# A gated linear attention with an expert layer on one core: logits made token by token, tables on GpSimd, the running state added by TensorE, first loads reordered

## The chip, the cores and the metric

The kernel runs on one core of one Trainium2 chip. Its time is the device time of one execution in microseconds (us), lower is better; the kernel before was run three times, and the median is given with the lowest and the highest. Beside these runs stands one execution taken by the profiler.

The engines are called PE (TensorE, matrix products; PEld its weight loads), DVE (VectorE), ACT (ScalarE), POOL (GpSimd) and SP (SyncE, which here only starts transfers).

## What is computed

An attention with a decaying state, and behind it a layer that sends each token to the one expert with the largest logit.

```
q, k, v, alpha: (4, 8, 768, 48)          batch, heads, sequence, width
for t in range(768):
    state = alpha[t][:, None] * state + outer(k[t], v[t])      # per batch and head
    y[t]  = q[t] @ state
x = y, tokens by (head, width): (3072, 384)
logits = x @ w_gate + modality_bias[modality_id]               # 8 experts
e = argmax(logits);  gate = softmax(logits)[e]
out[token] = gate * (relu(x[token] @ w1[e]) @ w2[e])           # 384 -> 1024 -> 384
```

## The kernel before, in words

**Chunks.** The tokens are cut into 24 chunks of 128 (NU), six for each of the four sequences (NC). A chunk holds all 8 heads. The host lays the inputs out: `turned` has keys, queries and decays with the width on the partitions (two heads side by side, 112 partitions, 1600 columns, 700 KB a chunk), and `rowsv` has the values with the tokens on the partitions, each head's 48 columns padded to 64 with zeros (256 KB a chunk).

**Loads.** `load` (L125) issues a chunk's two transfers on SP's queue. For chunk 0 the block comes in three parts (decays, keys, queries). Three chunks are loaded ahead (PF), there are four block buffers (TN) and six value buffers (VT).

**One step of the attention loop** (L812 to L844), step s of 24. The order is written out by hand for PE, DVE, ACT and POOL. Different chunks are in different stages:
- DVE: `decay(s)` (a scan over the decays backwards into the PSUM tile GF, L233, two small instructions, and keys times GF, L239, as `kh`), then `decay_back(s)` (a second scan, L243, and queries times GF, L245, as `qh`).
- PE and ACT: `natural(s-1)` turns the keys (L256), `rows(s-3)` turns the outputs into rows and stores them to `xd` (L326, L331), `state(s-2)` multiplies the queries with the state T1 carried in (L288), `scores(s-1)` makes keys times queries (L268), which ACT copies and POOL masks (L272, L273), `outputs(s-2)` multiplies the masked scores with the values (L295, ACT copy L303 to `yt`), `update(s-1)` makes keys times values (L313).
- `update` goes on with an ACT copy (L315), a POOL addition of the carried state T1 (L317), and a POOL multiplication by the chunk's decay, which gives the next T1 (L319).
- Every second step two chunks get their logits: `logits` (L338) multiplies the gate weights as the stationary operand, four narrow column groups, so that experts lie on partitions; ACT copies (L340); one step on `logits_rows` turns both back with two transposes (L346) and DVE sums the four groups into `L` (L348).

PSUM tiles named `tr` share three buffers in turn; `kv` (GF's name) and `y` have one, `sc` two. In the last part of the attention the logits use `kv` (`turns`) and the routing uses `sc` (`place`).

**Routing beside it.** `bias_table` (L201) makes the table `bt` of each token's bias from its modality, mostly on DVE, in pieces from step 5 on. In five groups of chunks (`GROUPS`: 0 to 5, 6 to 11, 12 to 15, 16 to 19, 20 to 23) `route_flow` (L398) adds the bias (L409), takes the largest logit (L410 to L414, giving the one-hot `oh`), counts with PE how many tokens before it went to the same expert (L417 to L424), and makes each token's slot: `r1`, `hr`, `lo`, `hi`, and the table `OL` of 128 columns a chunk (L437). After 16 and after 20 chunks `route_early` (L494) picks the fullest expert, has its weights loaded (`weights`, L618, four transfers of 768 KB on SP's queue), and looks up 256 of its tokens (`OHE`, L518 and L524; PE L531; `places`), which `gather` (L650) fetches on POOL's queue. These flows are generators; `advance()` runs one more piece of each flow at two places of a step: behind `decay` and behind `decay_back`.

**Hand-over.** After the loop the last scores, outputs and logits are interleaved by hand with the last pieces of routing and with the first products of the first expert (`first_inputs`, `first_unit`, L121).

**Experts.** Blocks of 256 or 512 tokens are multiplied with their expert's weights. Both operands are split into a high and a low part on ACT and DVE and multiplied in three products (L955 to L957 and L974 to L976), with weight loads and gathers beside it.

Of the kernel before, what the change touches and what calls it, by code (L numbers as in the profile page):

```python
# [21 lines left out]
P = 128  # L22
# [3 lines left out]
W = 64 + D  # L26
# [39 lines left out]
def attention_moe(ctx: ExitStack, tc: tile.TileContext, q, k, v, alpha, mid, wg, mb, w1, w2, turned, rowsv, small, out):  # L66
# [25 lines left out]
    for i in range(NV):  # L92
        t = ac.tile([P, H, 64], F32, name=f"vt{i}")
        VT.append(t)
# [29 lines left out]

    def load(i):  # L125
        if i:
            sp.dma_start(TN[i % NB], turned[i])
        else:
            for c in (slice(2 * KW, RW), slice(0, KW), slice(KW, 2 * KW)):
                sp.dma_start(TN[0][:, c], turned[0, :, c])  # L130
        sp.dma_start(VT[i % NV], rowsv[i])

    wgs = cp.tile([P, ND, E], F32, name="wgs")
    for i in range(PF):
        load(i)
# [24 lines left out]
    for i in range(3):  # L160
        t = ac.tile([W, NP, 64], F32, name=f"T1{i}")
        pool.memset(t[:, :, D:], 0.0)
        T1.append(t)
    bhi = ac.tile([P, 1], F32, name="bhi")
# [36 lines left out]
    def bias_table():  # L201
        mf = ac.tile([NU, P], F32, name="mf")
        vec.tensor_copy(mf, mi[:, :, 0])
        yield
        mp = ps.tile([P, NU], F32, name="sc", bufs=2)
        pe.transpose(mp, mf, ident[:NU, :NU])
        mt = ac.tile([P, NU], F32, name="mt")
        vec.tensor_copy(mt, mp)
        tmp = ac.tile([P, NU, E], F32, name="btt")
        for m in range(NM):  # L210
            yield
            sel = ac.tile([P, NU], F32, name=f"msel{m}")
            vec.tensor_scalar(sel, mt, float(m), None, op0=ALU.is_equal)
            vec.tensor_tensor(
# [5 lines left out]
            if m:  # L220
                vec.tensor_tensor(bt, bt, tmp, op=ALU.add)

# [83 lines left out]
    def update(i):  # L306
# [8 lines left out]
        act.copy(S1, kv)  # L315
        if i % NC > 0:
            pool.tensor_tensor(S1, S1, T1[i % 3][:, :, :D], op=ALU.add)  # L317
# [15 lines left out]
    def logits(i):  # L333

        lt = ps.tile([P, 2, P], F32, **turns)
        for n in range(NP):
            g, h = divmod(n, 2)
            pe.matmul(lt[32 * n : 32 * n + 32], wgp[:, g, h], st[i, "yt"][:, :, g, h], start=True, stop=True)  # L338
        ls = sb.tile([P, 2, P], F32, name="lts")
        act.copy(ls, lt)  # L340
        st[i, "l"] = ls

    def logits_rows(i):
        lp = ps.tile([P, 2, P], F32, **turns)
        for c in range(2):
            pe.transpose(lp[:, c], st[i, "l"][:, c], ident)  # L346
        z = slice(i - 1, i + 1)
        vec.tensor_reduce(L[:, z], lp.rearrange("p c (j e) -> p c e j", e=32)[:, :, :E], axis=AX.X, op=ALU.add)  # L348
# [880 lines left out]
```

## Time and profile before

| | |
|---|---|
| median of 3 runs | 363.36 us (361.44 to 364.71) |
| profiled execution, its own time | 362.08 us |
| its span, first to last instruction | 360.3 us |
| busy in the span: PE, PEld | 333.0 us, 288.9 us |
| busy in the span: DVE, ACT, POOL | 223.8 us, 177.7 us, 156.2 us |
| mean granted PE clock | 0.968 of full speed |
| first scan of the first step | 4.26 us |
| read from and written to HBM | 53.69 MB, 9.50 MB |

A row in order of time gives start, length, engine, line, operation, what it writes and reads, the shapes, how many instructions were merged, and in brackets how long the engine stood idle before it and what ended that. Merged rows overlap a little: an instruction's length reaches past the start of the next one, so distances between starts are what an engine needs. A row of a group gives the count, the busy time in us, the mean of one in ns, and idle time ahead of it. In the rows by slices each digit is a tenth of busy time in one of 40 equal slices of 9 us.

### The profile page before, as it was taken

How to read it: one execution, taken by the hardware profiler on the slowest of the kernel's cores; microseconds unless marked ns; L12 is line 12 of the kernel's file. 1: busy time of each engine (PE TensorE's matmuls, PEld its weight loads, DVE VectorE, ACT ScalarE, POOL GpSimd, SP SyncE). 2: the span in 40 equal slices, each digit the busy share in tenths (PEclk: the TensorE clock that was granted, in tenths of full speed). 3: DMA queues.
4: the chain of work that ended last, by engine and by line, in shares of the span. 5: the costliest groups of instructions: out<-in, count | busy, mean ns of one | idle time of the engine just before them, and what ended most of it. 6: DMA issues, size and time to landing. Idle time of an engine off the chain costs nothing. (4 is left out here: it accounts for less than half of the span.)

```text
span 360.3 us, 8600 instructions
## 1 busy us (share of the span) xinstructions
PE 333.0 (92%) x3378; PEld 288.9 (80%) x3378; DVE 223.8 (62%) x438; ACT 177.7 (49%) x344; POOL 156.2 (43%) x197
## 2 busy tenths in 40 slices
PE   6599889997986989998999999999999999999993
PEld 2487678675775868898988998899899888988992
DVE  5799999999999875978466226604560555036400
ACT  2477677684875554446355144515542544154410
POOL 8378366573835532075556127123702571120021
PEclk9589999998999699999999999999999999999998
DMA  8999998699792949779474336333641573110011
GB/s 227 256 258 285 274 284 227 197 277 241 222 253 67 313 151 308 258 254 318 142 243 147 109 104 225 94 126 133 196 132 67 159 253 90 46 44 6 1 45 51
DMA packets 29333, 63.78 MB, mean 177 GB/s; under 512 B 3369, under 2 KB 14792, under 8 KB 29284
## 3 DMA queue, kind: packets, MB, share of 16 engines
q1 hardware_dynamic: 25140, 53.40, 49.7%
q0 software_dynamic: 4000, 9.68, 7.9%
q8 instruction: 28, 0.46, 0.6%
q14 instruction: 21, 0.17, 0.2%
q10 hardware_dynamic: 144, 0.07, 0.1%
HBM read 53.69 MB, written 9.50 MB: 175 GB/s over the span
## 5 line engine op out<-in xcount | busy, mean ns | idle before, releaser
L921 POOL DMA_INDIRECT out_dram<-os,odx x23 | 23.5, 1020 | 102.9 <-ACT os L989 93.9
L955 PE MATMUL sc<-w2H,hH 128*128 128x384 f32 x192 | 65.2, 340 | 0.0
L957 PE MATMUL sc<-w2H,hL 128*128 128x384 f32 x192 | 64.3, 335 | 0.0
L956 PE MATMUL sc<-w2L,hH 128*128 128x384 f32 x192 | 64.3, 335 | 0.0
L799 DVE TENSOR_TENSOR w1L<-w1r,w1H 128x768 fp32r<-128x768 f32 x24 | 22.0, 956 | 65.2 <-ACT w1H L797 65.2
L273 POOL TENSOR_SCALAR_AFFINE_SELECT scT<-scT 128x512 f32<-128x512 f32 x48 | 38.5, 825 | 46.1 <-ACT scT L272 46.1
L974 PE MATMUL tr<-xH,w1H 128*128 128x512 f32 (+1 forms) x144 | 53.9, 374 | 0.0
L976 PE MATMUL tr<-xH,w1L 128*128 128x512 f32 (+1 forms) x144 | 53.6, 372 | 0.0
L975 PE MATMUL tr<-xL,w1H 128*128 128x512 f32 (+1 forms) x144 | 53.5, 372 | 0.0
L791 DVE SCALAR_TENSOR_TENSOR hL<-tr,hH 128x512 fp32r<-128x512 f32 x47 | 32.4, 689 | 30.8 <-ACT hH L789 30.8
L789 ACT ACTIVATE hH<-tr 128x512 fp32r<-128x512 f32 x47 | 28.1, 598 | 43.0 <-PE tr L976 41.7
L989 ACT ACTIVATE os<-sc,gg 128x384 f32<-128x384 f32 x23 | 13.4, 582 | 66.8 <-PE sc L957 40.7
L658 POOL DMA_INDIRECT gg<-gd,idx x25 | 27.1, 1083 | 26.7 <-DMA gd<-gs 19.7
L955 PEld LDWEIGHTS sc<-w2H,hH 128*128 128x128 f32 x192 | 36.1, 188 | 1.1 <-issue 1.0
L956 PEld LDWEIGHTS sc<-w2L,hH 128*128 128x128 f32 x192 | 36.1, 188 | 0.0
L957 PEld LDWEIGHTS sc<-w2H,hL 128*128 128x128 f32 x192 | 36.1, 188 | 0.0
L233 DVE TENSOR_TENSOR_SCAN kv<-tn,DR 112x512 f32<-112x512 f32 x24 | 32.6, 1357 | 5.1 <-DMA tn<-in_turned_dram 4.7
L272 ACT COPY scT<-sc 128x512 f32<-128x512 f32 x48 | 25.8, 589 | 18.9 <-PE sc L268 18.9
L268 PE MATMUL sc<-qh,kh 48*64 48x128 f32 x768 | 29.5, 290 | 4.7 <-DVE qh L245 2.9
L652 POOL DMA_INDIRECT xg<-xd,idx x25 | 26.7, 1067 | 14.8 <-DVE vals L488 8.1
L243 DVE TENSOR_TENSOR_SCAN kv<-tn,DF 112x512 f32<-112x512 f32 x24 | 31.4, 1309 | 0.3
L268 PEld LDWEIGHTS sc<-qh,kh 48*64 48x64 f32 x768 | 24.5, 145 | 8.0 <-DVE qh L245 3.2
(245 smaller groups left out, 599.1 us busy)
## 6 DMA issues: line engine op xcount, KB each, us to landing
tn<-in_turned_dram SPq DMA_DIRECT2D x23, 700.0 KB, 6.6
w1r<-in_moe_w_dram SPq DMA_DIRECT2D x16, 768.0 KB, 4.9
w2r<-in_moe_w_dram SPq DMA_DIRECT2D x16, 768.0 KB, 6.1
vt<-in_rowsv_dram SPq DMA_DIRECT2D x24, 256.0 KB, 6.7
xd<-xs SPq DMA_DIRECT2D x24, 192.0 KB, 6.4
tn<-in_turned_dram SPq DMA_DIRECT2D x2, 224.0 KB, 4.1
xg<-xd,idx POOLq DMA_INDIRECT x25, 4.3
gg<-gd,idx POOLq DMA_INDIRECT x25, 3.7
```

The costliest lines, as they stand in the source:

```text
L233: vec.tensor_tensor_scan(GF[:, ::-1], alphas(i, 1, KW + 1)[:, ::-1], DR[:, ::-1], 0.0, op0=ALU.mult, op1=ALU.max)
L243: vec.tensor_tensor_scan(GF, alphas(i, 0, KW), DF[i % 2], 0.0, op0=ALU.mult, op1=ALU.add)
L268: pe.matmul(pp[g][z, j], kh[r, j, z], qh[r, j], start=True, stop=True)
L273: pool.affine_select(s, s, [[0, NP], [1, P]], ALU.is_ge, 0.0, base=0, channel_multiplier=-1)
L789: act.activation(hH, hp, AF.Relu)
L791: vec.scalar_tensor_tensor(hL, hp, 0.0, hH.bitcast(F32), op0=ALU.max, op1=ALU.subtract)
L955: pe.matmul(op, hH[:, us] if f is None else hH[:, f, us], wH, start=first, stop=False)
L956: pe.matmul(op, hH[:, us] if f is None else hH[:, f, us], wL, start=False, stop=False)
L957: pe.matmul(op, hL[:, us] if f is None else hL[:, f, us], wH, start=False, stop=final)
L974: pe.matmul(hp, wH[:, d, fs], XH[:, d, :n], start=(d == 0), stop=False)
L975: pe.matmul(hp, wH[:, d, fs], XL[:, d, :n], start=False, stop=False)
L976: pe.matmul(hp, wL[:, d, fs], XH[:, d, :n], start=False, stop=(d == ND - 1))
```

## The change

- **Loads.** Chunk 0's block in parts as before; then chunk 1's decays and keys, chunk 0's values, chunk 1's queries, chunk 1's values, and then chunk 2 as a whole.
- **Values unpadded.** The host no longer pads; a chunk's values are 192 KB. The tile has 64 more columns, set to zero once by POOL (six small memsets). `outputs` still reads 64 columns for each head: the upper 16 are now the next head's values. They land in rows of the output tile that `rows` leaves out and for which the gate weights are zero.
- **Logits.** The output tile `yt` is the stationary operand, eight products of 128 columns by 8 in a group of two chunks; the result has tokens on partitions. ACT's copy, the two transposes and DVE's sum go. `logits_rows` is one DVE addition of the product and the bias into `L`, at the end of the same step. L409 goes. Each group of chunks starts one step earlier.
- **Tables.** `bias_table` runs once in step 1, its two copies on ACT and its five other instructions on POOL. `lo` is made as a float; in the groups 0 to 5, 6 to 11 and 12 to 15 `OL` is made by POOL, one instruction for a chunk.
- **State.** PE adds T1 by a product with the identity ahead of the eight key-value products, all into one PSUM group; POOL's addition L317 goes.
- **Where the pieces run.** A flow says with `yield PEQ` that its next piece begins on PE; such a piece is now put behind `scores` and ahead of `outputs`. The `gather` of an early expert stands directly behind its `places`. In the hand-over one `next(early)` goes, as the group of chunks 16 to 19 is one piece further.

```diff
+    def load_part(i, z):
+        c = (slice(0, KW), slice(KW, 2 * KW), slice(2 * KW, RW))[z]
+        sp.dma_start(TN[i][:, c], turned[i, :, c])
+    def load_rows(i):
+        sp.dma_start(VT[i % NV][:, :DM], rowsv[i])
     def load(i):
-        if i:
-            sp.dma_start(TN[i % NB], turned[i])
-        else:
-            for c in (slice(2 * KW, RW), slice(0, KW), slice(KW, 2 * KW)):
-                sp.dma_start(TN[0][:, c], turned[0, :, c])
-        sp.dma_start(VT[i % NV], rowsv[i])
+        sp.dma_start(TN[i % NB], turned[i])
+        load_rows(i)
-    for i in range(PF):
-        load(i)
+    for z in (2, 0, 1):
+        load_part(0, z)
+    load_part(1, 2)
+    load_part(1, 0)
+    load_rows(0)
+    load_part(1, 1)
+    load_rows(1)
+    load(2)
...
+    for t in VT:
+        pool.memset(t[:, DM:], 0.0)
...
     def bias_table():
-        vec.tensor_copy(mf, mi[:, :, 0])
-        yield
+        act.copy(mf, mi[:, :, 0])
         pe.transpose(mp, mf, ident[:NU, :NU])
-        vec.tensor_copy(mt, mp)
+        act.copy(mt, mp)
         for m in range(NM):
-            yield
-            vec.tensor_scalar(sel, mt, float(m), None, op0=ALU.is_equal)
-            vec.tensor_tensor(
+            pool.tensor_scalar(sel, mt, float(m), None, op0=ALU.is_equal)
+            pool.tensor_tensor(
...
             if m:
-                vec.tensor_tensor(bt, bt, tmp, op=ALU.add)
+                pool.tensor_tensor(bt, bt, tmp, op=ALU.add)
...
     def outputs(i):
-                vt[:, 2 * j + g],
+                vt[:, (2 * j + g) * D : (2 * j + g) * D + 64],
...
     def update(i):
+        if i % NC > 0:
+            pe.matmul(kv, ident[:W, :W], T1[i % 3][:, :, :D], start=True, stop=False)
         for h in range(H):
-            pe.matmul(kv[r, h // 2], kn[:, h // 2, r], vt[:, h, :D], start=True, stop=True)
+            pe.matmul(kv[r, h // 2], kn[:, h // 2, r], vt[:, h * D : (h + 1) * D], start=(i % NC == 0), stop=(i % NC == 0 or h >= H - 2))
         act.copy(S1, kv)
-        if i % NC > 0:
-            pool.tensor_tensor(S1, S1, T1[i % 3][:, :, :D], op=ALU.add)
...
     def logits(i):
-        lt = ps.tile([P, 2, P], F32, **turns)
-        for n in range(NP):
-            g, h = divmod(n, 2)
-            pe.matmul(lt[32 * n : 32 * n + 32], wgp[:, g, h], st[i, "yt"][:, :, g, h], start=True, stop=True)
-        ls = sb.tile([P, 2, P], F32, name="lts")
-        act.copy(ls, lt)
-        st[i, "l"] = ls
+        lp = ps.tile([P, 2, E], F32, **turns)
+        for c in range(2):
+            for n in range(NP):
+                g, h = divmod(n, 2)
+                pe.matmul(lp[:, c], st[i, "yt"][:, c, g, h], wgp[:, g, h, :E], start=(n == 0), stop=(n == NP - 1))
+        st[i, "l"] = lp
     def logits_rows(i):
-        lp = ps.tile([P, 2, P], F32, **turns)
-        for c in range(2):
-            pe.transpose(lp[:, c], st[i, "l"][:, c], ident)
         z = slice(i - 1, i + 1)
-        vec.tensor_reduce(L[:, z], lp.rearrange("p c (j e) -> p c e j", e=32)[:, :, :E], axis=AX.X, op=ALU.add)
+        vec.tensor_tensor(L[:, z], st[i, "l"], bt[:, z], op=ALU.add)
...
-    def route_flow(t0, t1):
+    def route_flow(t0, t1, side=False):
-        vec.tensor_tensor(L[:, s], L[:, s], bt[:, s], op=ALU.add)
         vec.tensor_reduce(mx[:, s], L[:, s], axis=AX.X, op=ALU.max)
         vec.tensor_tensor(ls[:, s], L[:, s], wide(mx), op=ALU.subtract)
+        if side:
+            yield
...
-        yield
+        yield PEQ
         rp = ps.tile([P, n, E], F32, **place)
...
-        vec.tensor_scalar(lo[:, s], r1[:, s], P - 1, None, op0=ALU.bitwise_and)
+        vec.scalar_tensor_tensor(lo[:, s], hr[:, s], -float(P), r1[:, s], op0=ALU.mult, op1=ALU.add)
-        vec.tensor_tensor(OL[:, s], over(ioh, P), wide(lo, P), op=ALU.is_equal)
+        if side:
+            for t in range(t0, t1):
+                pool.tensor_scalar(OL[:, t], ioh, lo[:, t : t + 1], None, op0=ALU.is_equal)
+        else:
+            vec.tensor_tensor(OL[:, s], over(ioh, P), wide(lo, P), op=ALU.is_equal)
...
     def route_early(s):
-        yield
+        yield PEQ
         cnt = ps.tile([P, E], F32, **place)
...
         weights(s, mete[0:1, s : s + 1])
-        yield
+        yield PEQ
         tp = ps.tile([P, 2], F32, **place)
...
         places(tp, slice(UE * s, UE * s + UE))
+        gather(s, early_cols(s), row(n))
...
+    def advance(spot):
+        for f in list(flows):
+            tag, seen = flows[f]
+            if (tag == PEQ) != (spot == PEQ) or seen == (now["s"], 2):
+                continue
+            go(f, spot)
...
         decay(s)
         if live(s - 1) and (s - 1) % NC < NC - 1:
             natural(s - 1)
         if live(s - 3):
             rows(s - 3)
-        if live(s - 4) and s % 2:
-            logits_rows(s - 4)
-        advance()
+            if (s - 3) % 2:
+                logits(s - 3)
+        advance(1)
         decay_back(s)
-        if s < NU - 1:
-            advance()
-        if s % 2:
-            groups(s - 4)
+        advance(2)
+        if live(s - 3) and (s - 3) % 2:
+            logits_rows(s - 3)
+            groups(s - 3)
         if s == 5:
-            start(bias_table())
             half_index()
-        if live(s - 3) and (s - 3) % 2:
-            logits(s - 3)
         guard(s)
         if live(s - 2):
             state(s - 2)
         if live(s - 1):
             scores(s - 1)
+        if s == 1:
+            bias_table()
+        advance(PEQ)
         if live(s - 2):
             outputs(s - 2)
         if live(s - 1):
             update(s - 1)
...
     next(early)
     logits(L0 - 2)
-    next(early)
     state(L0 - 1)
```

More of the change, by code (lines that the diff above doesn't have):

```diff
@@ L92, in attention_moe @@
     for i in range(NV):
-        t = ac.tile([P, H, 64], F32, name=f"vt{i}")
+        t = ac.tile([P, DM + 64], F32, name=f"vt{i}")
         VT.append(t)
@@ L202, in bias_table @@
         mf = ac.tile([NU, P], F32, name="mf")
-        vec.tensor_copy(mf, mi[:, :, 0])
-        yield
-        mp = ps.tile([P, NU], F32, name="sc", bufs=2)
+        act.copy(mf, mi[:, :, 0])
+        mp = ps.tile([P, NU], F32, name="tr", bufs=3)
         pe.transpose(mp, mf, ident[:NU, :NU])
         mt = ac.tile([P, NU], F32, name="mt")
-        vec.tensor_copy(mt, mp)
+        act.copy(mt, mp)
         tmp = ac.tile([P, NU, E], F32, name="btt")
         for m in range(NM):
-            yield
             sel = ac.tile([P, NU], F32, name=f"msel{m}")
-            vec.tensor_scalar(sel, mt, float(m), None, op0=ALU.is_equal)
-            vec.tensor_tensor(
+            pool.tensor_scalar(sel, mt, float(m), None, op0=ALU.is_equal)
+            pool.tensor_tensor(
                 tmp if m else bt,
@@ L358, in logits_pe @@
             pe.matmul(lp, xc[:, c], wgs[:, c], start=(c == 0), stop=(c == ND - 1))
-        vec.tensor_copy(L[:, i], lp)
+        vec.tensor_tensor(L[:, i], lp, bt[:, i], op=ALU.add)
     mx = cp.tile([P, NU], F32, name="mx")
@@ L379, in attention_moe @@
     r1 = cp.tile([P, NU], I32, name="r1")
-    lo = cp.tile([P, NU], I32, name="lo")
+    lo = cp.tile([P, NU], F32, name="lo")
     ls = cp.tile([P, NU, E], F32, name="ls")
@@ L389, in attention_moe @@
     turns = {"name": "tr", "bufs": 3}
+    PEQ = "pe"
     def route_begin():
@@ L749, in group_flow @@
     def group_flow(t0, t1):
-        yield from route_flow(t0, t1)
+        yield from route_flow(t0, t1, t1 < EARLY[-1])
         if t1 in EARLY:
@@ L753, in group_flow @@
             yield from route_early(e)
-            gather(e, early_cols(e), row(t1))
             if e == NA - 1:
@@ L759, in group_flow, with go @@
                     gather_gates(e, early_cols(e), row(t1))
-    flows = []
-    def advance():
+    flows, now = {}, {}
+    def advance(spot):
         for f in list(flows):
-            if next(f, f) is f:
-                flows.remove(f)
-    def start(f):
-        flows.append(f)
-        if next(f, f) is f:
-            flows.remove(f)
-    def finish():
-        while flows:
-            advance()
+            tag, seen = flows[f]
+            if (tag == PEQ) != (spot == PEQ) or seen == (now["s"], 2):
+                continue
+            go(f, spot)
+    def go(f, spot):
+        try:
+            flows[f] = (next(f), (now["s"], spot))
+        except StopIteration:
+            del flows[f]
     def live(i):
@@ L782, in groups @@
             if after == i:
-                start(group_flow(t0, t1))
+                go(group_flow(t0, t1), 2)
     hpool = {}
@@ L817, in attention_moe @@
             sp.dma_start(gd[MID : MID + 1], zr[:, 0:1])
+        now["s"] = s
         decay(s)
@@ L822, in attention_moe @@
             rows(s - 3)
-        if live(s - 4) and s % 2:
-            logits_rows(s - 4)
-        advance()
+            if (s - 3) % 2:
+                logits(s - 3)
+        advance(1)
         decay_back(s)
-        if s < NU - 1:
-            advance()
-        if s % 2:
-            groups(s - 4)
+        advance(2)
+        if live(s - 3) and (s - 3) % 2:
+            logits_rows(s - 3)
+            groups(s - 3)
         if s == 5:
-            start(bias_table())
             half_index()
-        if live(s - 3) and (s - 3) % 2:
-            logits(s - 3)
         guard(s)
@@ L1197, in laid_out @@
     turned[:, :, 2 * KW : 3 * KW] = a.reshape(NU, W, KW)
-    rowsv = np.zeros((NU, P, H, 64), np.float32)
-    rowsv[..., :D] = v.reshape(B, H, NC, P, D).transpose(0, 2, 3, 1, 4).reshape(NU, P, H, D)
+    rowsv = np.ascontiguousarray(v.reshape(B, H, NC, P, D).transpose(0, 2, 3, 1, 4)).reshape(NU, P, DM)
     small = np.zeros((P, P + NM * E), np.float32)
```

## The prediction

> **What bounds the kernel now.** I read the page first, then busy time by stretches, then VectorE's (DVE's) and TensorE's (PE's) instructions in order of time, then the groups by line and form. The page's slices:
>
> ```profile
> DVE  5799999999999875978466226604560555036400
> PEclk9589999998999699999999999999999999999998
> ```
>
> DVE is full from about 18 to 126 us; the granted PE clock (PEclk) is low in the second slice and dips twice more. Behind the attention the columns change places (length, PE, PEld, DVE, ACT, POOL busy):
>
> ```profile
> 130.00:140.00 10.00, 10.00 (x158) 7.80 (x155) 5.14 (x34) 4.71 (x10) 3.25 (x4) 1.00 0.43 133
> 140.00:150.00 10.00, 10.00 (x62) 8.29 (x60) 8.90 (x41) 3.93 (x8) 0.00 (x0) 1.00 0.83 296
> ```
>
> From 130 us PE never rests and DVE has room. So there are two stages, DVE-bound and then PE-bound, and they meet where the last attention step hands over. DVE, in order of time (start, length):
>
> ```profile
> 10.77 1.23 DVE L233 TENSOR_TENSOR_SCAN kv<-tn,DR 112x512 f32<-112x512 f32 x1 [2.30 <-DMA tn<-in_turned_dram]
> ...
> 15.19 1.23 DVE L233 TENSOR_TENSOR_SCAN kv<-tn,DR 112x512 f32<-112x512 f32 x1
> ...
> 19.31 1.34 DVE L233 TENSOR_TENSOR_SCAN kv<-tn,DR 112x512 f32<-112x512 f32 x1
> ...
> 124.57 0.23 DVE L348 TENSOR_REDUCE L<-tr 128x16 f32<-128x64 f32 x1 [0.95 <-PE tr L346]
> ...
> 126.22 0.69 DVE L245 TENSOR_TENSOR qh<-tn,kv 112x512 f32<-112x512 f32 x1
> ...
> 127.48 0.19 DVE L410 TENSOR_REDUCE mx<-L 128x4 f32<-128x32 f32 x1
> ...
> 128.94 0.33 DVE L414 TENSOR_TENSOR oh<-eq,m 128x32 bf16<-128x32 f32 x1
> ```
>
> From 15.19 to 19.31, 4.12 us, is one step of decay and decay_back with nothing between. The second step waited 2.30 us for its load. L348 waited 0.95 for PE once more near the end. The last step's product L245 ends at 126.22 + 0.69 = 126.9. PE around that point:
>
> ```profile
> 116.89 0.58 PE L531 MATMUL tr<-OHE,OL 128*128 128x2 f16 x16 [2.69 <-DVE OHE L524]
> ...
> 119.32 1.93 PE L268 MATMUL sc<-qh,kh 48*64 48x128 f32 x32
> ...
> 129.32 0.19 PE L417 MATMUL sc<-oh,tri 128*128 128x32 bf16 x1 [0.94 <-DVE oh L414]
> ...
> 130.60 1.05 PE L268 MATMUL sc<-qh,kh 48*64 48x128 f32 x32
> ```
>
> The last scores (L268, step 23) start at 130.60, 3.7 us after their operand was ready: PE is late, because it waited 2.69 us for OHE, then ran its scores in 1.93 us instead of 1.05, then waited 0.94 for a one-hot. From 130.60 to the end the work is a PE queue. So two things count: when DVE finishes step 23, and how late PE is then.
>
> **The change, part by part.** Before 126.9 on DVE:
>
> (1) First loads in order of use. Now step 1's alphas come with its whole 700 KB block, behind step 0's values. After, only alphas, keys and values parts stand before what each instruction needs. The 2.30 us wait should go, but step 2's block is then next: 258 + 229 + 229 + 258 + 229 + 197 + 229 + 197 + 717 KB = 2.54 MB must have landed before the third step, and it is wanted 2.3 us sooner than its 15.19. In the old order the second block, 1.69 MB into the queue, is there at 10.77; 0.85 MB more at the 0.25 to 0.28 MB/us of these rows
>
> ```profile
> GB/s 227 256 258 285 274 284 227 197 277 241 222 253 67 313 151 308 258 254 318 142 243 147 109 104 225 94 126 133 196 132 67 159 253 90 46 44 6 1 45 51
> ```
>
> is 3.2 us, so 13.9, against 15.19 − 2.30 = 12.9. I count a gain of 1.4, bounds 0.6 and 2.3. Values unpadded save 64 KB in each step of 717 + 262 + 197 KB (block, values, stored rows); no later scan waits for a load, so this only makes the faster pace possible: 1.11 MB in 4.3 us is 0.26 MB/us, what the slices show. If that cover were gone, each step would lose about 0.3 us.
>
> (2) Bias table, slot table and the bias add leave DVE:
>
> ```profile
> L437 DVE TENSOR_TENSOR OL<-ioh,lo 128x512 f16<-128x512 f16 x3 | 2.4, 792 | 0.0
> L437 DVE TENSOR_TENSOR OL<-ioh,lo 128x768 f16<-128x768 f16 x2 | 1.9, 947 | 0.0
> L409 DVE TENSOR_TENSOR L<-L,bt 128x32 f32<-128x32 f32 x3 | 1.2, 407 | 0.0
> L409 DVE TENSOR_TENSOR L<-L,bt 128x48 f32<-128x48 f32 x2 | 0.6, 302 | 0.0
> L214 DVE TENSOR_TENSOR bt<-msel,sm 128x192 f32<-128x192 f32 x1 | 0.7, 731 | 0.0
> L214 DVE TENSOR_TENSOR btt<-msel,sm 128x192 f32<-128x192 f32 x1 | 0.4, 359 | 0.0
> L221 DVE TENSOR_TENSOR bt<-bt,btt 128x192 f32<-128x192 f32 x1 | 0.4, 359 | 0.0
> L213 DVE TENSOR_SCALAR msel<-mt 128x24 f32<-128x24 f32 x2 | 0.3, 170 | 0.0
> ```
>
> Bias: 0.73 + 0.36 + 0.36 + 2 × 0.17 and two small copies at the same 0.17 are 2.1; starts overlap by some 0.05 each on DVE, so 1.8. Slot table: three of the five groups go to GpSimd (POOL), 2 × 0.95 + 0.8 = 2.7, 2.5 with overlap. The bias add moves into the instruction that empties the logits (a sum of 128x16 instead of L348's 0.23: no difference; bounds ±0.1 × 12), so its own instructions go: three ahead of 126.9, 2 × 0.30 + 0.41 = 1.0. The other two lie behind it, where PE binds.
>
> (3) Waits for the logits. L now reads the product directly, at the end of the step in which PE made it, half a step later than PE needs: the 0.95 goes, 1.0.
>
> (4) Against that, the group of chunks 16 to 19 starts one step earlier, so its arithmetic (127.48 to 128.94 + 0.33, 1.8 us with its longest three stretched) moves ahead of the last step: −1.4, bounds −1.1 and −1.8.
>
> Sum: 1.4 + 1.8 + 2.5 + 1.0 + 1.0 − 1.4 = 6.3; the last product ends at 120.6.
>
> (5) How late is PE then? The last two-chunk logits before it (chunks 20, 21) use the PSUM tile of the decay product (turns is kv, one buffer), so they can't start before 120.6; then come the state product and the scores. From PE's rows
>
> ```profile
> 73.27 0.64 PE L338 MATMUL tr<-yt,sm 128*32 128x256 f32 x8
> 74.15 1.10 PE L268 MATMUL sc<-qh,kh 48*64 48x128 f32 x32 [0.25 <-DVE qh L245]
> ...
> 77.10 0.60 PE L326 MATMUL tr<-ident,yt 128*128 128x128 f32 x4
> 77.53 0.38 PE L346 MATMUL tr<-ident,lts 128*128 128x128 f32 x2
> 77.85 0.67 PE L288 MATMUL y<-qh,T 64*64 64x128 f32 x16
> 78.58 1.10 PE L268 MATMUL sc<-qh,kh 48*64 48x128 f32 x32
> ...
> 139.28 1.46 PE L121 MATMUL tr<-xf,w1r 128*128 128x256 f32 x6
> ```
>
> the four 128x128 transposes of L326 take 0.43, 0.11 each. The new logits are eight such weight loads with 8 columns moved, 0.9 (bounds 0.6 and, at twice the price, 1.7); the old ones were 0.6 for L338 and 0.3 for L346: equal. State 0.5. So the last scores start at 120.6 + 0.9 + 0.5 = 122.0 and not at 130.60. The one-hot wait falls away, as that group is a step further on. Gain 8.6.
>
> (6) State added by PE: 16 products of identity with T1, 192 columns. L121 moves 256 columns in 1.46/6 = 0.24, so 0.18 each, 2.9 us; they lie beside DVE's work. PE's step from 74.15 to 78.58 is 4.43 with a wait in it, against DVE's 4.3 plus routing; the first and last step of each sequence skip state, update and transposes, so PE has room on average, little within a sequence. The PSUM result of the new logits holds one of three tr buffers until DVE reads it, which pushes rows and state (0.9 us) behind the end of DVE's step every second step: PE is late by about 1 us there, and it makes that up at the ends of sequences. Not on the path until PE is later than DVE's three buffers allow.
>
> (7) POOL. Its rows:
>
> ```profile
> L273 POOL TENSOR_SCALAR_AFFINE_SELECT scT<-scT 128x512 f32<-128x512 f32 x48 | 38.5, 825 | 46.1 <-ACT scT L272 46.1
> L319 POOL TENSOR_TENSOR T<-S,amin 112x192 f32<-112x192 f32 x20 | 18.5, 923 | 1.3
> L317 POOL TENSOR_TENSOR S<-S,T 112x192 f32<-112x192 f32 x16 | 11.8, 738 | 1.6 <-ACT S L315 1.4
> L467 POOL TENSOR_SCALAR dz<-ident,zc 128x52 f32<-128x52 f32 x1 | 0.4, 417 | 0.0
> ```
>
> It loses L317, 11.8 us, and gains five bias operations and 16 compares of 128x128; the nearest, L467, took 0.42 at 52 columns, so 0.3 to 1.2 each, I take 0.4 and 6.4 us: about as much as it loses. It is half idle, so selects and T1 come later by up to 2 us in three steps, less than the step that lies between. The gathers move up to directly behind their index; T1 of that step stands behind them, one POOL wait for PE of a microsecond or so, three steps before the end.
>
> DVE's scans feel POOL:
>
> ```profile
> L233 DVE TENSOR_TENSOR_SCAN kv<-tn,DR 112x512 f32<-112x512 f32 x24 | 32.6, 1357 | 5.1 <-DMA tn<-in_turned_dram 4.7
> L243 DVE TENSOR_TENSOR_SCAN kv<-tn,DF 112x512 f32<-112x512 f32 x24 | 31.4, 1309 | 0.3
> ```
>
> means of 1357 and 1309 against 1.23 for the unhindered ones make 48 × 0.10 = 5 us of stretch. What page SBUF — State Buffer of the Trainium skill says (section "Who interferes with whom") speaks against this change: a DVE instruction with two SBUF inputs and a GpSimd one that reads SBUF exclude each other, the one that starts second waiting for the whole of the first. The stretched scans here (up to 0.6 us over) agree. By it each compare could cost DVE one more wait.
>
> In rows: if every new POOL instruction (21) cost DVE its 0.4, that is 8.4 us; if the 16 lost ones gave back their share (11.8 of POOL's 68.8 us in these lines, times 5), a gain of 0.9. A scan is a third of DVE's time and one can be hit only once, so I take 0, range −3 to +1.
>
> Tail: PE gains on DVE there by 3.7 − 1.4 = 2.3 us, and DVE idles 4.9 of 10 us in that stretch, so DVE stays ahead. The first expert's weights are asked for two and a half DVE steps and the routing between them, some 13 us, before the last product; now it is 10.
>
> **Sum.** The profiled execution took 362.1 us with its 360.3 us span; 362.1 − 8.6 = 353.5. The runs shown have median 363.4, 1.3 above, which gives 354.8; I name 354.0. My bounds: startup −0.8/+0.9, contention −3/+1, logits price −0.8/+0.3, group −0.4/+0.3, bias add ±1.2; taken together about 350.5 to 358.
>
> **The rivals.** (A) PE cold at the hand-over. The PE rows with a wait ahead:
>
> ```profile
> 47.24 0.88 PE L268 MATMUL sc<-qh,kh 48*64 48x128 f32 x22 [1.25 <-issue]
> ...
> 84.58 0.20 PE L417 MATMUL tr<-oh,tri 128*128 128x48 bf16 x1 [2.45 <-DVE oh L414]
> ```
>
> After 1.25 us of waiting the clock stayed, after 2.45 and 2.69 it halved. The new order makes PE wait for DVE at the one-hot (half a DVE step, 2.1, plus 0.65 of routing, less the scores' 1.0: 1.75), for OHE (2.1 + 1.3 − 1.0 = 2.4, less PE's lateness of up to 1.5) and in front of the last logits (1.5). If a halving falls on the hand-over, the scores and what follows run at half pace for some 5 us: 2.5 to 3 lost, 357. For: the waits lie where these rows tell nothing, between 1.3 and 2.4. Against: early halvings are caught up. The Trainium skill (TensorE: Matmul & The Clock Gate, Part 1) has the clock fall only after an idle window of about 3.4 us, on a window that runs free. By that this rival has no chance; the rows halve after 2.45 us, so I leave it one.
>
> (B) POOL takes back on DVE what it relieves: 8.4 us as priced above, of which the forecast counts none, 361.9, no change. For: the stretch of the scans. Against: L317's 16 leave.
>
> (C) Slower: PE becomes the bound of the attention through the held tr buffer. Its place is rows, every second step; the point from which it decides is a wait of about 2 us, at which the clock halves. Twelve pairs times 2.5 us lost are 30. PE's room until the hand-over is 112 us (8.5 to 120.6), less 24 steps of 4.1 (4.43 without its wait, plus 0.18, less what sequence ends skip) and 3 of routing, plus 6 that lies behind: 16. So 14 over, 368. For: PE's 4.4 us per step. Against: I work out waits of 1 to 1.5 us there.
>
> (D) The change doesn't do what it says: DVE isn't the limit but loads are, at the faster pace. Then only waits and startup go, some half of it: 358.
>
> **Chances.** Forecast 0.68, A 0.13, B 0.06, C 0.04, D 0.09. The range is 349 to 360; B and C are left out. A measurement of this kernel tells about 1%, 3.6 us, from no change: faster 0.87 (forecast, A, two thirds of D), same 0.09 (B, the rest of D), slower 0.04 (C).
>
> **What would show it.** Right: no wait of the second scan or one under 1 us; no L437 or L409 rows of DVE in the first three groups; last product near 120.6, last scores within 2 us of it; from there on PE's rows as before. Wrong: scans' means over 1.45 us (B); halved clock in most slices up to 120 (C); DVE waiting for loads beyond the third step (D); last scores over 4 us behind the last product (A).

## The result, and the profile after

The change made the kernel slower, by 1%. Its median is 367.27 us (364.72 to 371.74, 15 runs) beside 363.36 us (360.01 to 365.83, 15 runs) for the kernel before on the same chip: a ratio of 1.0105, 95% interval 1.0069 to 1.0141. Forecast were 354.0 us, with 349 to 360 as the range. Ratios and intervals leave disturbed runs out, so that a ratio below can differ from that of two medians.

The profiled execution took 365.55 us with a span of 363.8. DVE and the granted PE clock in 40 slices of it:

```profile
DVE  5989889699779945969555326614460546035400
PEclk9589999999999999999999999999999999999999
```

The clock dips after the start are gone, and DVE now has gaps in the middle of the attention. Busy time by stretches after (length; PE, PEld, DVE, ACT, POOL with their instructions; clock; DMA share and GB/s):

```profile
20.00:130.00 110.00, 107.72 (x1955) 92.73 (x1955) 95.95 (x196) 71.68 (x161) 67.84 (x78) 1.00 0.75 223
130.00:140.00 10.00, 10.00 (x169) 8.80 (x170) 4.25 (x27) 4.40 (x10) 2.55 (x5) 1.00 0.19 37
140.00:150.00 10.00, 10.00 (x67) 8.60 (x67) 6.48 (x37) 2.62 (x5) 1.52 (x2) 1.00 1.02 366
```

and the first of these stretches in the kernel before:

```profile
20.00:130.00 110.00, 96.94 (x1895) 79.22 (x1894) 104.46 (x213) 74.79 (x174) 65.20 (x79) 0.95 0.85 243
```

DVE lost 8.5 us of work, as intended. PE gained 10.8 and is busy for 107.7 of 110 us at the full clock. The attention was bound by DVE and is bound by PE. DVE after, in order of time:

```profile
8.65 1.32 DVE L241 TENSOR_TENSOR_SCAN kv<-tn,DR 112x512 f32<-112x512 f32 x1
13.03 1.23 DVE L241 TENSOR_TENSOR_SCAN kv<-tn,DR 112x512 f32<-112x512 f32 x1
...
52.06 0.69 DVE L253 TENSOR_TENSOR qh<-tn,kv 112x512 f32<-112x512 f32 x1
...
69.74 0.17 DVE L352 TENSOR_TENSOR L<-tr,bt 128x16 f32<-128x16 f32 x1 [3.04 <-PE tr L347]
...
101.56 0.17 DVE L352 TENSOR_TENSOR L<-tr,bt 128x16 f32<-128x16 f32 x1 [3.04 <-PE tr L347]
...
128.97 0.69 DVE L253 TENSOR_TENSOR qh<-tn,kv 112x512 f32<-112x512 f32 x1
```

The third scan starts at 13.03 where it started at 15.19: the loads gave 2.2 us. Then DVE waits for PE's logits (L352), twice for 3.04 us, and the last product (L253, the old L245) ends at 129.66, against 126.9 before and 120.6 forecast. PE after:

```profile
54.17 0.58 PE L320 MATMUL tr<-T,ident 112*112 112x192 f32 x2
54.68 0.67 PE L323 MATMUL tr<-vt,knat 128*64 128x48 f32 x16
...
56.15 1.85 PE L347 MATMUL tr<-sm,yt 128*128 128x8 f32 x16
57.93 0.67 PE L296 MATMUL y<-qh,T 64*64 64x128 f32 x16
58.42 1.05 PE L276 MATMUL sc<-qh,kh 48*64 48x128 f32 x32
...
64.26 0.44 PE L303 MATMUL y<-scT,vt 128*64 128x128 f32 x4 [0.21 <-POOL scT L281]
...
133.28 1.05 PE L276 MATMUL sc<-qh,kh 48*64 48x128 f32 x32
```

Three things are to be read here. A pair's logits (L347) hold PE from 56.15 to 57.93, 1.78 us. The state sum (L320) holds it from 54.17 to 54.68, 0.51 us. And the scores at 58.42 use the product that DVE ended at 52.06 + 0.69 = 52.75: PE is 5.7 us behind, where in the kernel before the scores at 74.15 waited for their product. The last scores start at 133.28, not at 130.60 and not at 122.0. The groups (count, busy, mean ns of one, idle time ahead):

```profile
L347 PE MATMUL tr<-sm,yt 128*128 128x8 f32 x160 | 18.5, 251 | 0.0
L320 PE MATMUL tr<-T,ident 112*112 112x192 f32 x32 | 9.7, 385 | 1.2 <-POOL T L327 1.2
L352 DVE TENSOR_TENSOR L<-tr,bt 128x16 f32<-128x16 f32 x10 | 1.7, 172 | 8.7 <-PE tr L347 8.7
L446 POOL TENSOR_SCALAR OL<-ioh,lo 128x128 f16<-128x128 f16 x16 | 16.4, 1043 | 0.6 <-DVE lo L442 0.4
L241 DVE TENSOR_TENSOR_SCAN kv<-tn,DR 112x512 f32<-112x512 f32 x24 | 31.2, 1298 | 2.9 <-DMA tn<-in_turned_dram 2.6
L251 DVE TENSOR_TENSOR_SCAN kv<-tn,DF 112x512 f32<-112x512 f32 x24 | 31.6, 1315 | 0.6
```

The code issues 8 products for a pair's logits and one for a state sum; the counts (160 for ten pairs, 32 for 16 sums) show two PE instructions for each. A compare on POOL takes 1.04 us, 16 of them 16.4. DVE waits 8.7 us in all for the products of the logits (L352). The scans' means, 1298 and 1315 ns, were 1357 and 1309 before.

### The profile page after: what moved, and what is told of

Same layout as the page of the kernel before. It is cut to its first block, busy times and chain, and to the rows that moved or that the text cites. A ratio compares the mean times of both kernels' runs of the same rounds, so it can differ in the third digit from the quotient of the medians.

```text
span 363.8 us, 8791 instructions
## 1 busy us (share of the span) xinstructions
PE 348.4 (96%) x3482; PEld 307.5 (85%) x3482; DVE 216.7 (60%) x423; ACT 175.2 (48%) x334; POOL 162.8 (45%) x208
## 5 line engine op out<-in xcount | busy, mean ns | idle before, releaser
L670 POOL DMA_INDIRECT gg<-gd,idx x25 | 26.1, 1042 | 26.8 <-DMA gd<-gs 19.8
L664 POOL DMA_INDIRECT xg<-xd,idx x25 | 28.0, 1118 | 11.1 <-issue 4.6
L241 DVE TENSOR_TENSOR_SCAN kv<-tn,DR 112x512 f32<-112x512 f32 x24 | 31.2, 1298 | 2.9 <-DMA tn<-in_turned_dram 2.6
L251 DVE TENSOR_TENSOR_SCAN kv<-tn,DF 112x512 f32<-112x512 f32 x24 | 31.6, 1315 | 0.6
L986 PEld LDWEIGHTS tr<-xH,w1L 128*128 128x128 f32 x144 | 27.1, 188 | 4.7
L985 PEld LDWEIGHTS tr<-xL,w1H 128*128 128x128 f32 x144 | 27.1, 188 | 4.6
```

Source lines behind the costliest of these rows:

```text
L241: vec.tensor_tensor_scan(GF[:, ::-1], alphas(i, 1, KW + 1)[:, ::-1], DR[:, ::-1], 0.0, op0=ALU.mult, op1=ALU.max)
L251: vec.tensor_tensor_scan(GF, alphas(i, 0, KW), DF[i % 2], 0.0, op0=ALU.mult, op1=ALU.add)
L664: pool.indirect_dma_start(xg[x][:, u], None, xd[0:rows], IOA(idx[:, c : c + 1], 0), bounds_check=rows - 1, oob_is_err=False)
L985: pe.matmul(hp, wH[:, d, fs], XL[:, d, :n], start=False, stop=False)
L986: pe.matmul(hp, wL[:, d, fs], XH[:, d, :n], start=False, stop=(d == ND - 1))
```

## The experiments

Two theories stood at the start. The first, price: the new logits and the state sum cost PE two to three times the forecast, and PE became the bound. The second, compares: six compares in a row on POOL keep masks and carried state back, and PE waits for them. The ratios below are against the kernel before, of the same chip. e1 to e4 ran on one chip, e5 to e8 and e13 to e16 on a second, e9 to e12 on a third, e17 on a fourth, so that between these groups only ratios are compared.

| kernel | ratio | 95% interval |
|---|---|---|
| the change | 1.0105 | 1.0069 to 1.0141 |
| e1: change, old logits | 1.0215 | 1.0079 to 1.0351 |
| e2: change, state on POOL | 1.0092 | 1.0024 to 1.0161 |
| e3: change, both | 1.0128 | 1.0045 to 1.0212 |
| e4: change, slot tables on DVE | 1.005 | 1.0004 to 1.0095 |
| e5: change, old logits, state on POOL, slot tables on DVE | 0.9997 | 0.9956 to 1.0038 |
| e6: change, old logits, slot tables on DVE | 0.9875 | 0.9833 to 0.9917 |
| e15: e6 again | 0.9873 | 0.9817 to 0.9929 |
| e7: change, state on POOL, slot tables on DVE | 0.9953 | 0.9919 to 0.9988 |
| e8: before, new loads, unpadded values, bias table off DVE | 0.9902 | 0.9866 to 0.9938 |
| e9: before, slot tables on POOL | 1.0332 | 1.0276 to 1.0389 |
| e10: before, state on PE | 1.0006 | 0.997 to 1.0041 |
| e11: e8, state on PE | 0.9937 | 0.9903 to 0.997 |
| e12: before, new logits | 1.017 | 1.0109 to 1.0231 |
| e13: before, two groups' compares on POOL, one a step | 1.0022 | 0.9981 to 1.0063 |
| e14: e6, two groups' compares on POOL, one a step | 0.9993 | 0.9955 to 1.0031 |
| e16: before, new logits, slot tables on POOL | 1.0414 | 1.0345 to 1.0484 |
| e17: e6, first sequence's state on POOL | 0.9922 | 0.9891 to 0.9954 |

**Parts taken back one by one (e1 to e4).** Old logits are the `logits` and `logits_rows` of before: the products at the spot of the changed kernel, the two transposes, DVE's sum, a small DVE addition of the bias and the start of the routing's next group behind the scores:

```
-                pe.matmul(lp[:, c], st[i, "yt"][:, c, g, h], wgp[:, g, h, :E], start=(n == 0), stop=(n == NP - 1))
+            pe.matmul(lt[32 * n : 32 * n + 32], wgp[:, g, h], st[i, "yt"][:, :, g, h], start=True, stop=True)
...
+            pe.transpose(lp[:, c], st[i, "l"][:, c], ident)
```

> The changed kernel, with only the logits made the old way again (gate weights stationary, ACT copy, two transposes, sum on DVE, bias added by a small DVE instruction), the transposes behind the scores. Theory T1 (PE became the bound, because each new logits pair costs 16 PE instructions at 0.11 us, 1.78 us against 0.9): PE loses some 10.7 us of work in 12 pairs, DVE becomes the bound again near 121 to 123 us, so the time falls from 367 to about 358 to 360. Rival T2 (the slot compares on POOL, 6.2 us in a row, hold up masks and state and so PE): those stay, so the time falls by 3 us at most, to 364 or more.

For the state:

```
-        if i % NC > 0:
-            pe.matmul(kv, ident[:W, :W], T1[i % 3][:, :, :D], start=True, stop=False)
...
+            pool.tensor_tensor(S1, S1, T1[i % 3][:, :, :D], op=ALU.add)
```

> The changed kernel, with only the carried state added by POOL again. T1: the 16 identity products cost PE 0.51 each, 8.2 us; PE stays close to the bound, the time falls by 6 to 8 us, to about 359 to 361. T2: POOL has even more to do behind its compares (16 x 0.74 us), the time does not fall, 366 to 369.

Both at once:

> The changed kernel with old logits and the state added by POOL; loads, bias table, slot compares on POOL, unpadded values and the places of the routing pieces stay new. T1: PE's work is that of the kernel before, DVE binds the attention, the last product ends near 121 us; the prediction's own figure, 354 to 356. T2: the slot compares still hold up the masks, 362 or more.

And the slot tables:

```
-        if side:
-            for t in range(t0, t1):
-                pool.tensor_scalar(OL[:, t], ioh, lo[:, t : t + 1], None, op0=ALU.is_equal)
-        else:
-            vec.tensor_tensor(OL[:, s], over(ioh, P), wide(lo, P), op=ALU.is_equal)
+        vec.tensor_tensor(OL[:, s], over(ioh, P), wide(lo, P), op=ALU.is_equal)
```

> The changed kernel, with only the slot tables of the first three groups made by DVE again. T1: DVE has room beside a bound PE, so its 2.6 us cost little, and PE's short waits for masks and state (about 1.6 us) go: 365 to 368. T2: the compares were the cause: 360 to 362.

The first alone falls: with either or both of the dear PE parts gone the time stayed above before (1.0215, 1.0092, 1.0128). The second alone does not carry it either: without the compares the time came down by half a per cent, and even that is at the edge of the noise (the intervals overlap). The third kernel's profile shows what the spared PE time turned into. POOL's row of compares, the products behind the masks, and PE's waits (in all, times, longest):

```profile
55.04 6.36 POOL L451 TENSOR_SCALAR OL<-ioh,lo 128x128 f16<-128x128 f16 x6 [0.75 <-DVE lo L447]
61.36 2.15 POOL L281 TENSOR_SCALAR_AFFINE_SELECT scT<-scT 128x512 f32<-128x512 f32 x2
```

```profile
PE y L303 <- POOL scT L281: 6.2, 2, 3.7
PE tr L547 <- DVE OHE L540: 2.9, 1, 2.9
PE tr L429 <- DVE oh L426: 2.3, 3, 1.5
```

Work was exchanged for waiting: the masks start 6.4 us late, and PE, no longer behind, stands for 6.2 us in two places.

**Parts taken back together (e5 to e7) and the gains alone (e8).** The edits are those above; e8 is the kernel before with the new `load_part` and `load_rows`, the order of first loads, the unpadded values, and the changed `bias_table` called behind the scores of step 1.

> The changed kernel with three parts undone at once: old logits (weights stationary, transposed back), the state added by GpSimd, the slot tables of the first groups on VectorE. Kept are the new loads, the unpadded values, the bias table off VectorE, the earlier groups and the new places of the routing's products behind the scores. Theory PE-and-GpSimd (the two together made the loss: 10.7 + 5.2 us of TensorE work, and compares of 1.03 us ahead of masks and state sums): both are gone, so 354 to 358, 4 to 8 below the kernel before. Rival, places (what costs is where the routing's products now stand, behind the scores, where TensorE waits for one-hots and then runs at half pace, and that the logits are read at the end of VectorE's step): 361 to 365, and the profile shows waits of over 1.5 us ahead of those products.

> The changed kernel with old logits and the slot tables of the first groups on VectorE; the state sum stays on TensorE (16 x 0.51 us). Theory PE-and-GpSimd: with GpSimd free, each us of TensorE work counts, so this stands between the run with only the slot tables undone (ratio 1.005) and the run with all three undone; 356 to 360. Rival, places: 361 to 365.

> The changed kernel with the state sum on GpSimd and the slot tables of the first groups on VectorE; the new logits stay (1.78 us of TensorE a pair). Theory PE-and-GpSimd: 358 to 362, more than with the old logits since 10.7 us of TensorE work stay rather than 5.2. Rival, places: 361 to 365. If the new logits spare VectorE more than they cost TensorE: under 357.

> The kernel before with only the first loads in order of use, the values unpadded and the bias table on ScalarE and GpSimd; logits, state, slot tables and the order of routing as before. The prediction's steps 1 and 2 give 2.1 us (second scan 8.65 for 10.77 in the changed kernel) and 1.8 us on VectorE's path: if VectorE's end carries to the end of the kernel, 357 to 359. Rival: VectorE's earlier end is lost to TensorE's lateness at the hand-over (waits and half pace there): 360 to 362.

The change and e1 to e7 are all eight combinations of the three parts:

| logits, state sum | compares on POOL | slot tables on DVE |
|---|---|---|
| new, PE | 1.0105 (the change) | 1.005 (e4) |
| old, PE | 1.0215 (e1) | 0.9875 (e6) |
| new, POOL | 1.0092 (e2) | 0.9953 (e7) |
| old, POOL | 1.0128 (e3) | 0.9997 (e5) |

The compares cost something in each row, from 0.5% (not clear of the noise) to 3.4% with the old logits and the state on PE. With the compares off POOL and the state sum on PE the logits decide: 1.005 falls to 0.9875 when only they are undone as well (e4 to e6), 6.3 us. With the state sum on POOL they decide nothing that can be measured (e7 against e5). Undoing the state sum as well as the logits loses the gain again (e5, 0.9997), against what I expected; e5 lies in the range of its rival, places. The state sum on PE is thus worth 1.2% with the old logits, and costs 1.0% with the new ones (e4 against e7): neither part has a price of its own, it is the two together that PE has no room for. e5's waits of PE

```profile
PE tr L429 <- DVE oh L426: 4.3, 4, 1.5
PE tr L334 <- DVE L L356: 2.3, 2, 1.2
PE tr L264 <- DVE L L356: 1.8, 1, 1.8
```

beside those of e15, the same kernel with the state on PE,

```profile
PE tr L429 <- DVE oh L426: 1.6, 3, 0.9
PE tr L264 <- DVE L L356: 1.1, 1, 1.1
PE tr L543 <- DVE OHE L536: 1.0, 1, 1.0
```

say the same as e3's: what PE doesn't work, it waits. e8 shows that the safe parts are worth 1.0%, 3.6 us, near what the prediction had for the loads and the bias table (1.4 + 1.8 = 3.2), and between the range of its theory and that of its rival. In its profile the last scores start 3.9 us earlier than before, but at half pace, behind a wait for a one-hot, as the rival of e8 had it:

```profile
125.10 0.19 PE L425 MATMUL sc<-oh,tri 128*128 128x32 bf16 x1 [2.85 <-DVE oh L422]
...
126.72 1.95 PE L276 MATMUL sc<-qh,kh 48*64 48x128 f32 x32
```

The granted clock is 0.50 to 0.58 from 126.0 to 129.5 us there, some 1.7 us lost.

**Each part alone, on the kernel before (e9, e10, e12), and e8 with the state on PE (e11).** The slot tables alone:

> The kernel before with one edit: the slot tables of the first three groups on GpSimd, 16 compares of 128x128. Theory compares: six of them in a row are 6.2 us of GpSimd ahead of the masks, TensorE then waits for masks twice for 2 to 4 us in each of two groups, and VectorE's 2.5 us do not pay for it: 364 to 370, slower by 0.5 to 2%. Rival (the compares hurt only in the changed kernel, where TensorE has no room to catch up): 360 to 363, no change or a little faster.

The state alone, and with e8:

> The kernel before with one edit: the state added by TensorE (16 x 0.51 us) in place of GpSimd's sums (16 x 0.74). Theory room: TensorE was busy 97 of 110 us, so 8 us fit, and GpSimd's 11.8 us fewer give VectorE shorter scans: 358 to 361. Rival (each us of TensorE counts, since it is late at the hand-over): 365 to 370.

> The kernel before with first loads in order of use, values unpadded, bias table on ScalarE and GpSimd, and the state added by TensorE; logits, slot tables and the places and times of the routing as before. If the new places and the earlier groups cost by themselves (old logits and GpSimd state with the new places: ratio 0.9997; with the old places: 0.9902), this is below the run with old logits, VectorE slots and the new places (ratio 0.9875): 354 to 357. Rival (places do not matter once TensorE is busier): 357 to 360, a ratio of 0.984 to 0.99.

The new logits alone (emptied by `vec.tensor_copy(L[:, z], st[i, "l"])`, right behind the products):

> The kernel before with one edit: logits with tokens on partitions (16 TensorE instructions of 0.111 us a pair in place of 16 for the product and 2 transposes), emptied by a VectorE copy at the end of the same step, with the bias added in the routing as before. Theory price: 0.9 us a pair more on TensorE, and VectorE waits for them: 365 to 369. Rival room: TensorE has 13 us free, ScalarE's copy and the transposes go: 361 to 364.

The compares alone cost 3.3%, 12 us, three times what the whole change lost and more than was expected. POOL in the profile of that kernel, its group of compares, and PE behind it:

```profile
60.76 6.21 POOL L439 TENSOR_SCALAR OL<-ioh,lo 128x128 f16<-128x128 f16 x6 [3.40 <-DVE hi L436]
66.92 2.20 POOL L273 TENSOR_SCALAR_AFFINE_SELECT scT<-scT 128x512 f32<-128x512 f32 x2
```

```profile
L439 POOL TENSOR_SCALAR OL<-ioh,lo 128x128 f16<-128x128 f16 x16 | 16.4, 1039 | 13.1 <-DVE hi L436 13.1
```

```profile
68.59 2.14 PE L295 MATMUL y<-scT,vt 128*64 128x128 f32 x16 [6.10 <-POOL scT L273]
...
102.44 2.13 PE L295 MATMUL y<-scT,vt 128*64 128x128 f32 x16 [5.88 <-POOL scT L273]
...
124.22 2.13 PE L295 MATMUL y<-scT,vt 128*64 128x128 f32 x16 [3.19 <-POOL scT L273]
```

These rows show POOL taking its instructions in the order of the code. It first stands for DVE's routing (3.40 us here, 13.1 in all three groups), then works 6.21 us, and only then comes to masks whose copy ACT had ended at 63.67. PE waits 6.10, 5.88 and 3.19 us, 15.2 in all, and after each wait runs at half pace (16 products in 2.14 us where 1.09 is usual). In the changed kernel the same 16 compares take the same 16.4 us, but POOL waits for `lo` for 0.6 us only and PE for masks for 0.4 us in all (one of the two waits at 64.26 above): PE, and so the masks, are 5.7 us behind DVE there, and the row of compares falls into that lag. The state alone costs and gains nothing (1.0006): PE had room for it, so that the rival fell, but the 1 to 4 us that the theory expected did not come either. e11 is no better than e8 (0.9937 and 0.9902) and above both of its expected ranges.

The new logits alone cost 1.7%, 6.2 us. PE was free for 13 us of 110 in the kernel before; in e12, with 1.78 us a pair, it is free for 2.5:

```profile
20.00:130.00 110.00, 107.49 (x1955) 96.82 (x1953) 101.73 (x216) 70.95 (x163) 67.17 (x79) 0.94 0.85 243
```

In the profiled execution of e12 (366.22 us) the last scores start at 131.41, only 0.8 us later than before; the other 3.3 of its 4.1 us lie behind them, where PE was the bound already. The last pair's logits stand there (0.9), PE waits 1.9 us for gathered tokens where it was 1.1, and it runs at half pace right behind the last scores:

```profile
131.41 1.05 PE L268 MATMUL sc<-qh,kh 48*64 48x128 f32 x32
132.40 1.85 PE L295 MATMUL y<-scT,vt 128*64 128x128 f32 x16
```

The granted clock is 0.50 to 0.57 from 132.5 to 136.0 us, some 1.7 us lost, and no wait of PE in the ten us before was over 0.26. So e12 shows a price of the new logits, but not that it is paid through PE's room: that 6.2 us are so near the 6.3 of e4 to e6 is chance as far as is shown.

**Number of compares, or their row (e13, e14), the sum (e16).** One compare a step, behind that step's `update`:

```
+        if t1 <= 12:
+            late.extend(range(t0, t1))
+        else:
+            vec.tensor_tensor(OL[:, s], over(ioh, P), wide(lo, P), op=ALU.is_equal)
...
+    def slot():
+        if late:
+            t = late.pop(0)
+            pool.tensor_scalar(OL[:, t], ioh, lo[:, t : t + 1], None, op0=ALU.is_equal)
...
         if live(s - 1):
             update(s - 1)
+        slot()
```

What is left in `late` then is made in `route_early`, ahead of the first lookup.

> The kernel before with the slot tables of the first two groups on GpSimd, but one compare of 128x128 in each step, behind the sums of that step, in place of six in a row; the third group's table stays on VectorE. Theory row (what costs is that masks and state sums stand behind six compares): 360 to 363, as before or a little below. Rival amount (each compare costs by itself, through GpSimd's time or VectorE's scans): 366 or more, since 12 of the 16 compares are still there.

> The best kernel so far (the changed one with old logits and slot tables on VectorE) with the first two groups' tables again on GpSimd, one compare in each step. Theory row: VectorE loses 1.9 us and nothing waits, so 1 to 2 us below the run without them (ratio 0.983 to 0.9875). Rival amount: ratio 0.995 or more.

> The kernel before with the new logits and the slot tables of three groups on GpSimd, both at the old places (alone: ratios 1.017 and 1.0332). Theory two limits (TensorE, late through its own work, does not also wait for the masks): less than the sum of both, 374 to 377. Rival (the losses add): 380 or more.

Spread out, the 12 compares on the kernel before cost nothing that can be measured (1.0022), and the wait is gone, though they take as long:

```profile
L447 POOL TENSOR_SCALAR OL<-ioh,lo 128x128 f16<-128x128 f16 x12 | 12.6, 1049 | 0.0
```

So it is the row and its place ahead of the masks, not the number. But they gain nothing either, and in e6's frame they lose 1.2% (e14), so the theory of the row explains the loss and not all of the compares' price. Some of it is a wait again: in e14's profile the last compare stands behind a pair of masks (2.15 us), and the lookup for the first expert waits for it:

```profile
111.66 0.29 PE L555 MATMUL tr<-OHE,OL 128*128 128x2 f16 x5 [2.16 <-POOL OL L459]
```

e14's last scores start 1.2 us behind e15's (128.88 and 127.72); the rest of its 1.2%, 4.4 us, is open. e16 lost 4.1% beside 3.3 + 1.7 = 5.0, at the edge of what was expected (376.8 us). The intervals are too wide to tell whether the losses overlap or add.

**The best version (e15, e17).**

> The changed kernel with old logits and slot tables on VectorE once more (ratio 0.9875 before), beside the run with the compares spread. If the new places and earlier groups are worth something with the state on TensorE, this stays below the 0.9937 of the old places: 357 to 360.

The change without its logits and its compares beats both kernels twice (0.9875 and 0.9873, 4.6 us below before). Its profile shows one loss at the start:

```profile
18.76 0.98 PE L320 MATMUL tr<-T,ident 112*112 112x192 f32 x2 [0.96 <-POOL T L327]
```

```profile
29.61 0.22 DVE L356 TENSOR_REDUCE L<-tr 128x16 f32<-128x64 f32 x1 [3.73 <-PE tr L354]
```

For e17 the first sequence's sums went back to POOL:

```
-        if i % NC > 0:
+        if i % NC > 0 and i >= NC:
             pe.matmul(kv, ident[:W, :W], T1[i % 3][:, :, :D], start=True, stop=False)
...
+        if 0 < i < NC:
+            pool.tensor_tensor(S1, S1, T1[i % 3][:, :, :D], op=ALU.add)
```

> The best kernel (old logits, slot tables on VectorE, state on TensorE; ratios 0.9875 and 0.9873) with the state of the first sequence alone left to GpSimd. In its profile TensorE runs at half pace until 21 us, waits 0.96 us for T there, is 4 us late by 29 us, and VectorE waits 3.7 us for logits. If that loss reaches the end: 1 to 3 us less, a ratio of 0.979 to 0.985. Rival (TensorE makes it up later, and GpSimd's sums stretch the scans): 0.986 to 0.99.

It was not faster (0.9922, outside both expected ranges). In its profile that wait of DVE is gone and the last scores start 1.3 us earlier than e15's (126.46 and 127.72), but the execution was only 0.6 us shorter (359.35 and 359.96); what takes the rest back is open.

## Why the prediction was wrong, step by step

- **(1) and the bias table of (2) held.** Startup gave 2.2 us for 1.4 forecast, and e8 has the two together at 3.6 us. DVE did lose 8.5 us of work, but **(3) failed**: where a wait of 0.95 was to go, DVE waits 8.7 us for L347, because PE comes late.
- **(5) failed first: "equal".** The new logits were priced as eight weight loads at the 0.11 us of a transpose. The price of one instruction was right (1.78 / 16 = 0.111); the count was half. The prediction's own rows showed it: four products are "x8" in the row of L338 and three are "x6" in that of L121, while four transposes are "x4" in that of L326. My bound "at twice the price, 1.7" held the truth, but was carried into the range for one pair (+0.8), not for twelve. With the compares off POOL, undoing it is worth 6.3 us while the state sum is on PE (e4 to e6) and nothing while it is on POOL (e7, e5); alone on the old kernel it costs 6.2 (e12).
- **(6) failed in its size:** 0.51 us a state sum for 0.18. L121's 0.24 was one of two instructions; I took a product for an instruction again, and I scaled it from 256 to 192 columns, where the row shows no fall (0.25). "PE has room on average" was true of the kernel before (e10: no change) and false of the change, since logits and state together are 16 × 0.51 + 12 × 0.9 = 19 us of new PE work, most of it in the stretch where PE stood free for 13 of 110 us.
- **(7) failed in its size and its place:** 1.04 us a compare for 0.4, and "selects and T1 come later by up to 2 us" was 6.2. The row was priced by its sum against what POOL loses; it should have been read as one wait, 6 times the price, ahead of a queue in order, with POOL's own wait for its operand in front. In the change itself taking the compares back is worth only half a per cent, as PE is late anyway; alone they cost 12 us. The scans show no stretch from the compares (1298 and 1315 ns), as forecast, though the reason given was off: one scan is a third of a DVE step, but a step has two (2 × 1.3 of 4.3 us).
- **The hand-over.** "The last scores start at 122.0" fell with these three. Of what was then counted on, an earlier hand-over is not paid in full either: from the last scores to the end the kernel before needs 362.08 − 130.60 = 231.5 us, the change 365.55 − 133.28 = 232.3, e8 361.14 − 126.72 = 234.4. Of the 2.9 us that e8 loses there, its half pace explains some 1.7 and longer waits for gathered tokens 0.7 (1.8 against 1.1). These are single executions.
- **The rivals.** C named the right engine and had 0.04: PE became the bound, but by its work, at full clock, with no halving and no held buffer. That its 368 lies beside the measured 367.27 is luck: its 14 us came from halvings behind a held buffer, which did not happen. A and B fell in the change: no clock dip after the start, scans of 1298 and 1315. D fell: no scan waits for a load in the middle. A's mechanism, half pace after a wait, is real in e9, where PE does wait, and in e8 at the very hand-over. None of the four signs of being wrong appeared in the change: what failed had no rival of its own.

Of the 13.3 us between 354.0 and 367.27, the ratios 1.0105 and 0.9873 put 8.4 on logits and compares together (0.0232 × 363.36); the other 4.9 are gains of the sum that even the version without them doesn't have. Open is also what the new places of the routing and the earlier groups are worth: with the state on POOL they go with a loss (e8 to e5, 0.9902 to 0.9997), with the state on PE with a gain (e11 to e6, 0.9937 to 0.9875). One thing the profiles do show: before the last scores PE waits for a one-hot for 2.85 us in e8, and in the change and e15, where that group is a step further, it does not.

## What to carry to other kernels

Count instructions in the trace before pricing a new product: the count in a row of the same type, divided by the products that the code issues, is the first factor of the price. When work is given to an engine that isn't the bound, read it as a row in an order: what stands behind it, and for whom, and how long the row itself waits for its operand. And before trusting that two engines have room, add all new work to the one that is nearly full; relieving it where another engine holds the data back only turns work into waits.

## What the runs showed of the hardware

- An f32 product is two PE instructions here, a transpose one. With 8 columns moved each takes 0.111 us, as a transpose of 128 columns does: at this size the columns don't set the pace. That the 128x128 weights do, which both have, is the nearest reading and not shown apart. With 192 columns one takes 0.25, with 256 (L121) 0.24.
- A compare of 128x128 on POOL takes 0.6 us or 1.6 and once 2.1 in e13, and 1.04 or 1.05 on average in the change, e9 and e13:

```profile
60.12 0.61 POOL L447 TENSOR_SCALAR OL<-ioh,lo 128x128 f16<-128x128 f16 x1
...
65.00 1.57 POOL L447 TENSOR_SCALAR OL<-ioh,lo 128x128 f16<-128x128 f16 x1
```

  DVE did 128x768 in 0.95, 0.16 for as much, in an instruction of another form. What page GPSIMD Engine Reference of the Trainium skill (section "Engine selection") advises, elementwise work on a tile to VectorE and not to GpSimd, these rows bear out; its "roughly line-rate" for one input they don't.
- PE ran at half pace after waits of 3.19 to 6.10 us (e9), of 2.85 (e8) and of 1.79 (e5, granted clock 0.50 from 108 to 111 us); after waits of 1.51 it did so in e3 and not in e5; in the change, where it waits for 0.53 us at most, the granted clock of the stretch from 20 to 130 us is 1.00, against 0.95 in the kernel before. In e12 it ran at half pace with no wait over 0.26 in the ten us before. So the length of the last wait alone does not tell, and the 2 us that the prediction's rival C went by are not borne out as a point where it turns.
